# Attention of the first two blocks written as one pipeline ahead of the layers' loop

## The chip, the cores and the metric

One core of a Trainium2 chip runs the whole program. The metric is the device time of one execution in microseconds (us): 1756.26 us is the median of three runs of the kernel before (1754.75 to 1756.78). TensorE (PE) multiplies matrices, VectorE (DVE) and ScalarE (ACT) do elementwise work and read PSUM, GpSimd (POOL) does elementwise work in SBUF, SyncE (SP) issues most DMAs.

## The reference, cut to what matters

```python
# q, k, v: (batch 8, heads 8, seq 576, head_dim 64)
q_s = exp(q - max over d); q_s = q_s / (sum over d + 1e-9)
k_s = exp(k - max over s); k_s = k_s / (sum over s + 1e-9)
kv = einsum('bhsd,bhse->bhde', k_s, v)
x = einsum('bhsd,bhde->bhse', q_s, kv)      # -> (4608 tokens, 512)
h = relu(x @ w_in); x2 = (h * h) @ w_out    # d_ff 2048
xn = x2 / rms(x2) * rms_g
out = (silu(xn @ w_gate) * (xn @ w_val)) @ w_out2   # d_ff 1536
```

The keys' softmax runs over the sequence, the queries' over the 64 elements of a head. The weights come as 64-bit floats and are converted on the chip to fp32; most products are made of three fp32r passes on operands split into a high part and a remainder.

## The kernel before, in words

Tokens are cut into nine blocks of 512 (`NB`), heads into four pairs (`NP`, called heads `hp` below). Block j needs the attention of batch j, and of batch j - 1 for its first tokens, since a batch has 576. For each head of a block the attention does: load k, q, v; keys: maximum over the sequence (`a_kmax`, a reduction on VectorE, then `a_kt`, `a_mc`, `a_kb` to bring it across partitions with two transposes on TensorE), subtraction (`a_ksub`, VectorE), exponential (`a_kexp`); queries: `a_qmax`, `a_qsub` (GpSimd for block 0, else VectorE), `a_qexp`, `a_qsum`, `a_qn`, four transposes (`a_qT`) and a split into two parts; `a_kv` multiplies keys and values (ten fp32 products, twenty instructions), `a_kvf` normalizes, a split makes `kvd`, and `a_x` gives the transposed x in three fp32r passes, which is split again for the layers (for blocks 0 and 1 by `split_by_pe`, with a product with minus the identity).

The first layer pair of a block runs over 16 units c (`FF1`): `p1_h` multiplies x with w_in's piece c (12 matmuls of 512 columns into `ps_h`), `p1_r` does relu and square on ScalarE, `p1_hi` and `p1_lo` split the result, and `p1_B`, two units later, multiplies it with w_out's piece c (12 matmuls into `acc`). Units run in the order `units`, block after block; the second layers of all blocks follow. For c of `AHEAD` = 8 and more, block 1's `p1_h` runs in block 0's unit, with the same weights.

`tick` (line 379) converts the weights as a pipeline of jobs: load (SP queue), `d_words` (ScalarE: two conversions `s` and `n`), `d_float` (three VectorE operations on `t`), `d_split` (ScalarE high part, VectorE remainder), and writes most pieces back to DRAM (`wd`) over ScalarE's queue; later units load them into a ring of seven tiles `ws` (`feed`). Eight pieces stay in SBUF (`w`). The w_in and w_out pieces are all converted during block 0.

The order: block 0's attention is written out as a string of steps (lines 1062 to 1070), with four ticks in it; block 1's attention is spread over block 0's units by `A_STEPS`; that of the later blocks over the units of the block before by `HALVES`, in half units, and block 2's starts in the second part of block 0. Before unit 16 the instructions of an engine may be reordered by the scheduler; from unit 16 on (`pinned`) they stand in program order. PSUM has eight banks: four `acc`, two `h`, two `a`.

Of the kernel before, what the change touches and what calls it, by code (L numbers as in the profile page):

```python
# [40 lines left out]
def attention_moe_kernel(  # L41
# [12 lines left out]
    nc = tc.nc  # L54
# [60 lines left out]


    turns = {"a": 0, "so": 0, "d": 0, "t": 0}

    def a_ps(j, hp, name):
        if j == 0:  # L120
            return ps_acc.tile([P, 512], F32, tag=f"acc{hp}", name=name)
        turns["a"] += 1
        return ps_a.tile([P, 512], F32, tag=f"a{turns['a'] % 2}", name=name)
# [84 lines left out]
    AHEAD = 8  # L208

    def ahead(j, key):  # L210
        return j == 1 and key[0] == "i" and key[1] >= AHEAD
# [41 lines left out]
    def d_words(key):  # L253
# [115 lines left out]
    for c in range(FF1):  # L369
        due["i", c] = c - 2.5  # L370
        due["o", c] = c
# [29 lines left out]
    def a_tile(j, hp, shape, tag, dtype=F32, bufs=2):  # L401
        if j > 0 or hp < 2:
            bufs = {"qT": 1, "kt": 3}.get(tag, bufs)
            return pools["a"].tile([P, *shape], dtype, tag=tag, name=tag, bufs=bufs)
        return pools["s"].tile([P, *shape], dtype, tag=f"{tag}{hp}", name=f"{tag}0", bufs=1)
# [110 lines left out]
    def a_kexp(j, hp):  # L516
# [3 lines left out]
        ke = pools["a"].tile([P, SF + 1, 2, D], F32, tag="ke", name="ke", bufs=1)  # L520
# [43 lines left out]
    def a_qT(j, hp):  # L564
        ps = a_ps(j, hp, "ps_q")
# [6 lines left out]
        if j > 1:  # L572
            qTs[j, hp] = ps
            return
        qT = a_tile(j, hp, [2, T], "qT", F32R)
        if j == 0 and hp + 1 < NP:
            split_by_pool(qT, ps)
        else:
            split(qT, ps, j)
        qTs[j, hp] = qT  # L580
# [17 lines left out]
    def a_kv(j, hp):  # L598
        if j >= B:
            return  # L600
        ps = a_ps(j, hp, "ps_kv")
# [14 lines left out]

    def a_kvd(j, hp):
        a_kvf(j, hp)
        if j < B:
            split(kvd[j % 2][hp], kvs.pop((j, hp)), j)  # L620
# [10 lines left out]
    def a_kvf(j, hp):  # L631
# [7 lines left out]
        f = pools["a"].tile([P, P], F32, tag="kvf", name="kvf")  # L639
# [10 lines left out]
    def a_kvn(j, hp):  # L650
        a_kv(j, hp)
        a_kvd(j, hp)

    def a_x(j, hp):
# [4 lines left out]
        for b, lo, hi in ((j - 1, 0, p0), (j, p0, P)):  # L659
            if lo == hi:  # L660
# [6 lines left out]
                j > 1 or lo == 0,  # L667
                True,
                j,
                j < 2,  # L670
            )
        if j < 2:
            xts[j, hp] = xp.tile([P, 2, T], F32R, tag="x", name="x")
            split_by_pe(xts[j, hp], ps, j)
        else:
            xts[j, hp] = ps
# [23 lines left out]
    def p1_A(j, c):  # L700
        if not ahead(j, ("i", c)):
            kept[j, c] = p1_h(j, c)
            if j == 0:
                kept[j, c] = p1_r(kept[j, c], gp, 2)
        if j == 0 and c >= AHEAD:
            kept[1, c] = p1_r(p1_h(1, c), pools["r"], FF1 - AHEAD)
        if not ahead(j, ("i", c)):
            used(("i", c))

    def p1_hi(j, c):  # L710
        r = kept.pop((j, c))
        if j > 0 and not ahead(j, ("i", c)):
# [287 lines left out]
    for j in range(1, NB):  # L1000
        for hp in range(NP):
            for n, (at, f) in enumerate(A_STEPS if j == 1 else HALVES):
                if j == 1:
                    at = 2 * ((-6, -4, -2, 0)[hp] + at) + 1
                else:
                    at += (j - 1) * 2 * FF1 - 11 + 2 * FF1 // NP * hp
# [184 lines left out]
```

## Time and profile before

| | us |
|---|---|
| median of three runs | 1756.26 |
| the profiled execution | 1756.28 |
| its span, first to last instruction | 1754.3 |
| TensorE busy in the span | 1713.2 |
| VectorE busy | 1065.3 |
| ScalarE busy | 766.4 |

The span is the time from the first to the last instruction of the profiled execution; 2.0 us of its time lie around it. Busy times of TensorE count a matmul from start to its modelled end, so that a chain of matmuls is measured from start to start. An operation is named by its output and inputs, `out<-in`; all operations stand on line 34 (a helper), so they are told apart by their tiles: `ps_h` and `acc` are the layers' PSUM tiles, `ps_kt`, `ps_kb`, `ps_kv`, `ps_q`, `ps_x` the attention's, `t`, `s`, `n`, `raw` the weights' conversion, `ws` and `w` weights.

### The profile page before, as it was taken

The page shows a single profiled execution, that of the slowest core. Times are in us where ns is not written, and L with a number is a line of the kernel's source. Part 1 is how long each engine was busy: PE and PEld are TensorE (multiplying, and loading weights), DVE is VectorE, ACT ScalarE, POOL GpSimd, SP SyncE. Part 2 cuts the span into 40 slices and gives each one's busy share as a digit, 9 for nine tenths or more (in the row PEclk, how much of TensorE's full clock was granted, in tenths as well). Part 3 has the DMA queues.
Part 4 walks back from the last instruction along what each step waited for, and adds up shares of the span by engine and source line. Part 5 has one row for each costly group of instructions (what it writes and reads, how often), then busy time and mean ns, then how long its engine had stood idle before and what let it go on. Part 6 is the DMA issues. An engine that isn't in the chain of part 4 may idle for free.

```text
span 1754.3 us, 22975 instructions
## 1 busy us (share of the span) xinstructions
PE 1713.2 (98%) x8338; PEld 1412.2 (81%) x8338; DVE 1065.3 (61%) x1866; ACT 766.4 (44%) x1351; POOL 151.3 (9%) x166
## 2 busy tenths in 40 slices
PE   5899999999999999999999999999999999999998
PEld 3678888878888887888888888888888888888997
DVE  7986465556656555432465887657766775756444
ACT  4677434455555455543544335232532343223121
POOL 2000000222323232220000000000000000000000
PEclk9999999999999999999999999999999999999999
DMA  6777657779888887766556567666766666666885
GB/s 186 241 273 283 195 156 228 244 224 301 269 272 279 279 254 241 231 204 222 173 179 209 188 199 258 198 209 200 252 205 208 201 213 218 209 200 193 291 302 199
DMA packets 184511, 398.41 MB, mean 227 GB/s; under 512 B 57424, under 2 KB 96336, under 8 KB 183248
## 3 DMA queue, kind: packets, MB, share of 16 engines
q1 hardware_dynamic: 156368, 356.05, 62.5%
q10 hardware_dynamic: 28032, 40.90, 6.7%
q8 instruction: 67, 1.10, 0.3%
q14 instruction: 44, 0.36, 0.1%
HBM read 337.12 MB, written 59.77 MB: 226 GB/s over the span
## 4 chain that ended last, share of the span: by engine, by line
PE 94%; DVE 3%; DMA 1%; issue 1%; ACT 1%; SPq 0%; POOL 0%; ACTq 0%; DVEq 0%; POOLq 0%
PE acc L34 38%; PE ps_h L34 21%; PE ps_x L34 10%; PE ps_y L34 8%; PE ps_v L34 8%; PE ps_w L34 4%; PE ps_kv L34 2%; PE ps_q L34 1%; DVE t L34 1%; DMA vt<-in_v 1%; DVE mk L34 0%; DVE kt L34 0%; DVE qs L34 0%; DMA x2d<-e 0%; DMA kt<-in_k 0%
## 5 line engine op out<-in xcount | busy, mean ns | idle before, releaser
L34 PE MATMUL ps_h<-x,ws 128*128 128x512 f32 x1296 | 322.2, 398 | 4.0 <-DVE ws L34 2.6
L34 PE MATMUL acc<-g,ws 128*128 128x512 f32 x1296 | 315.2, 392 | 0.4 <-DVE ws L34 0.4
L34 PE MATMUL acc<-ws,g 128*128 128x512 f32 x1296 | 313.4, 390 | 1.0 <-ACT g L34 0.9
L34 PEld LDWEIGHTS ps_h<-x,ws 128*128 128x128 f32 x1296 | 240.9, 190 | 56.2 <-DVE ws L34 3.9
L34 PEld LDWEIGHTS acc<-g,ws 128*128 128x128 f32 x1296 | 241.9, 188 | 52.8 <-DVE ws L34 1.5
L34 PEld LDWEIGHTS acc<-ws,g 128*128 128x128 f32 x1296 | 241.4, 188 | 51.3 <-ACT g L34 2.1
L34 ACT ACTIVATE g<-r 128x512 fp32r<-128x512 f32 x252 | 158.7, 631 | 230.5 <-DVE r L34 226.0
L34 DVE TENSOR_TENSOR g<-r,g 128x512 fp32r<-128x512 f32 x252 | 172.5, 684 | 122.0 <-ACT g L34 120.3
L34 ACT ACTIVATE r<-ps_h 128x512 f32<-128x512 f32 x144 | 85.8, 597 | 243.0 <-PE ps_h L34 239.8
L34 PE MATMUL ps_y<-xo,ws 128*128 128x512 f32 (+1 forms) x720 | 168.6, 369 | 0.0
L34 PE MATMUL ps_v<-xo,ws 128*128 128x512 f32 (+1 forms) x720 | 168.4, 368 | 0.0
L34 PE MATMUL ps_x<-xo,ws 128*128 128x512 f32 (+1 forms) x720 | 167.5, 368 | 0.5 <-ACT p L34 0.5
L34 PEld LDWEIGHTS ps_x<-xo,ws 128*128 128x128 f32 x720 | 127.9, 188 | 24.4 <-ACT p L34 0.9
L34 PEld LDWEIGHTS ps_v<-xo,ws 128*128 128x128 f32 x720 | 127.7, 188 | 23.4
L34 PEld LDWEIGHTS ps_y<-xo,ws 128*128 128x128 f32 x720 | 126.4, 189 | 24.2 <-DVE sa L34 1.5
L34 PE MATMUL ps_h<-x,w 128*128 128x512 f32 x432 | 109.4, 402 | 0.9 <-DVE w L34 0.9
L34 PE MATMUL acc<-g,w 128*128 128x512 f32 x432 | 104.9, 392 | 1.0 <-ACT w L34 1.0
L34 PEld LDWEIGHTS ps_h<-x,w 128*128 128x128 f32 x432 | 81.2, 192 | 18.5 <-DVE w L34 1.3
L34 PEld LDWEIGHTS acc<-g,w 128*128 128x128 f32 x432 | 80.5, 188 | 18.7 <-ACT w L34 1.4
L34 ACT ACTIVATE r<-r 128x512 f32<-128x512 f32 x144 | 90.2, 631 | 3.7
L34 DVE TENSOR_TENSOR u<-ps_y,p 128x512 f32<-128x512 f32 (+1 forms) x120 | 76.0, 633 | 23.0 <-PE ps_y L34 21.5
L34 ACT ACTIVATE sg<-silu 128x512 f32<-128x512 f32 (+1 forms) x90 | 51.5, 585 | 83.6 <-DVE silu L34 83.4
(105 smaller groups left out, 1835.2 us busy)
## 6 DMA issues: line engine op xcount, KB each, us to landing
ws<-wd_t SPq DMA_DIRECT2D x210, 512.0 KB, 4.1
ws<-wd_u SPq DMA_DIRECT2D x108, 512.0 KB, 4.3
ws<-wd_o SPq DMA_DIRECT2D x96, 512.0 KB, 4.4
ws<-wd_i SPq DMA_DIRECT2D x89, 512.0 KB, 4.2
wd_t<-so ACTq DMA_DIRECT2D x84, 256.0 KB, 4.5
raw<-in_w_out SPq DMA_DIRECT2D x28, 512.0 KB, 4.7
raw<-in_w_gv SPq DMA_DIRECT2D x24, 512.0 KB, 5.7
x2d<-e SPq DMA_DIRECT2D x36, 256.0 KB, 2.9
```

Source lines behind the costliest of these rows:

```text
L34: ins = f(*args, **kw)
```

## The change

The attention of blocks 0 and 1 is done for all eight heads before the layers' loop, in nine written rounds, in program order on every engine (`pinned` is true from the start). Keys are transposed on TensorE (`s_kT`, four transposes), their maximum is a reduction along the free axis straight from PSUM (`s_km`), the exponential takes it as a bias (`s_ke`), and the result is transposed back (`s_kb`, five transposes) and copied to SBUF (`s_kc`). The 64 keys left over of each batch are transposed for all heads at once (`s_left`). Queries are copied once in fp32 (`s_qc`, no split), x is one fp32 product with the fp32 kv (`s_x`), and its remainder is made by the product with minus the identity (`s_xn`). The queries' subtraction moves to GpSimd for block 1 too. Block 2's boundary part gets its `kvd` split in units 8 to 11 of block 0.

Then block 0's units run by `unit_of_0`, with two ticks in each; block 1's first layer runs beside ten of them instead of eight (`AHEAD`). Each tick's split is cut in `d_hi` and `d_lo`, with the conversion of another weight between; the conversion `s` of w_in's pieces moves from ScalarE to VectorE. Weights are due one unit later. Block 2's attention starts two half units later. Keys of blocks 0 and 1 are loaded in pieces of 256 bytes and in the order p, c, h, d. Five ticks lie in the rounds 3 to 7. The rest of the program is the same.

```diff
-    AHEAD = 8
+    AHEAD = (1, 3, 5, 7, 9, 11, 12, 13, 14, 15)
...
-        if key[0] in ("i", "o"):
+        if key[0] == "o":
             se.activation(out=s, in_=hi, func=AF.Copy, scale=2.0**-112)
         else:
-            ge.tensor_scalar(
+            eng = ve if key[0] == "i" else ge
+            eng.tensor_scalar(
...
-    def d_split(key):
+    def d_hi(key):
         t = slot_tile(key) if key in res1 else ring_tile()
-        w_split(t, floats.pop(key), ve)
+        se.activation(out=t[:, 0], in_=floats[key], func=AF.Copy)
+        wt[key] = t
+
+    def d_lo(key):
+        t = wt[key]
+        ve.tensor_tensor(
+            out=t[:, 1], in0=floats.pop(key), in1=t[:, 0].bitcast(F32), op=ALU.subtract
+        )
         if key not in res1:
-            send(key, t, 2)
-        wt[key] = t
+            send(key, t, 1)
...
-        due["i", c] = c - 2.5
-        due["o", c] = c
+        due["i", c] = c - 1.5
+        due["o", c] = c + 0.5
...
-    def tick():
+    def tick(between=None):
         n = ticks[0]
-        for stage, ahead in ((d_split, 0), (d_float, 1), (d_words, 2), (d_load, 4)):
-            if 0 <= n - 4 + ahead < len(jobs):
-                key = jobs[n - 4 + ahead]
-                if key is None:
-                    continue
-                if stage == d_split and n - 4 + ahead >= NJ1:
-                    stage = d_quad
-                stage(key)
+        w1 = ((d_hi, 0), (d_float, 1), (d_lo, 0), (d_words, 2), (d_load, 4))
+        w2 = ((d_quad, 0), (d_float, 1), (d_words, 2), (d_load, 4))
+        for stage, ahead in w1 if n < NJ1 + 4 else w2:
+            if between and stage == d_words:
+                between()
+            if 0 <= n - 4 + ahead < len(jobs) and jobs[n - 4 + ahead] is not None:
+                stage(jobs[n - 4 + ahead])
         ticks[0] += 1
         if n < NJ1 + 4:
...
+    A_BUFS = {"kt": (3, 1), "qt": (3, 1), "vt": (2, 2), "qn": (2, 0), "ke": (1, 1), "qT": (1, 0)}
...
-        eng = ve if j > 0 else ge
+        eng = ve if j > 1 else ge
...
+    def s_left(j):
+        ps = lefts[j] = s_ps("h", "ps_l")
+        kl = kls.pop(j)
+        for hp in range(NP):
+            src = kl[:, hs_(hp), :].rearrange("p h d -> p (h d)")
+            te.transpose(ps[:, hp * SR : (hp + 1) * SR], src, ident[0:SR, 0:SR])
+        lmax[j] = s_tile([P, NP], "lm", 2)
+        ve.tensor_reduce(
+            out=lmax[j],
+            in_=ps[:, 0 : NP * SR].rearrange("p (n s) -> p n s", n=NP),
+            axis=AX.X,
+            op=ALU.max,
+            negate=True,
+        )
+
+    def s_kT(j, hp):
+        ps = kT[j, hp] = s_ps(f"acc{hp % 2}", "ps_kt")
+        kt = s_chunks(kts.pop((j, hp)))
+        for c in range(SF):
+            src = kt[:, c].rearrange("p h d -> p (h d)")
+            te.transpose(ps[:, c * P : (c + 1) * P], src, ident)
+
+    def s_km(j, hp):
+        m = s_tile([P, 2], "m", 2)
+        ve.tensor_reduce(out=m[:, 0:1], in_=kT[j, hp], axis=AX.X, op=ALU.max, negate=True)
+        ve.tensor_tensor(
+            out=m[:, 1:2], in0=m[:, 0:1], in1=lmax[j][:, hp : hp + 1], op=ALU.min
+        )
+        mks[j, hp] = m
+
+    def s_ke(j, hp):
+        ek = eks[j, hp] = s_tile([P, S], "ek", 2)
+        m = mks.pop((j, hp))[:, 1:2]
+        se.activation(out=ek[:, 0 : SF * P], in_=kT.pop((j, hp)), func=AF.Exp, bias=m)
+        se.activation(
+            out=ek[:, SF * P : S],
+            in_=lefts[j][:, hp * SR : (hp + 1) * SR],
+            func=AF.Exp,
+            bias=m,
+        )
+
+    def s_kb(j, hp):
+        ek = eks.pop((j, hp))
+        ps = kT[j, hp] = s_ps(f"acc{hp % 2}", "ps_kb")
+        for c in range(SF):
+            te.transpose(ps[:, c * P : (c + 1) * P], ek[:, c * P : (c + 1) * P], ident)
+        ps = kvs[j, hp] = s_ps("a0", "ps_kv")
+        te.transpose(ps[0:SR, P : 2 * P], ek[:, SF * P : S], ident)
+
+    def s_kc(j, hp):
+        ke = kes[j, hp] = a_tile(j, hp, [SF + 1, 2, D], "ke")
+        se.activation(
+            out=ke[:, 0:SF].rearrange("p c h d -> p (c h d)"), in_=kT.pop((j, hp)), func=AF.Copy
+        )
+        ve.tensor_copy(
+            out=ke[0:SR, SF].rearrange("p h d -> p (h d)"), in_=kvs[j, hp][0:SR, P : 2 * P]
+        )
+
+    def s_qc(j, hp):
+        f = qfs[j, hp] = s_tile([P, T], "qf", 2)
+        se.activation(out=f, in_=qTs.pop((j, hp)), func=AF.Copy)
+
+    def s_x(j, hp):
+        ps = xts[j, hp] = s_ps(f"acc{2 + hp % 2}", "ps_x")
+        qf = qfs.pop((j, hp)).rearrange("p (c t) -> p c t", c=NG)
+        p0 = min(j * OFF // NG, P)
+        view = ps.rearrange("p (c t) -> p c t", c=NG)
+        for b, lo, hi in ((j - 1, 0, p0), (j, p0, P)):
+            if lo < hi:
+                te.matmul(
+                    view[:, :, lo:hi],
+                    kvs[b, hp],
+                    qf[:, :, lo:hi],
+                    start=lo == 0,
+                    stop=True,
+                    skip_group_check=True,
+                )
+
+    def s_xh(j, hp):
+        split_hi(xts, (j, hp), xp.tile([P, 2, T], F32R, tag="x", name="x"))
+
+    def s_xn(j, hp):
+        t, ps = xts[j, hp]
+        te.matmul(ps, neg_r, t[:, 0], start=False, stop=True, skip_group_check=True)
+
+    def s_xl(j, hp):
+        t, ps = xts[j, hp]
+        se.activation(out=t[:, 1], in_=ps, func=AF.Copy)
+        xts[j, hp] = t
...
+    def p1_ahead(c):
+        kept[1, c] = p1_h(1, c)
+        used(("i", c))
+
+    def p1_ahead_r(c):
+        kept[1, c] = p1_r(kept[1, c], pools["r"], len(AHEAD))
...
-                    at += (j - 1) * 2 * FF1 - 11 + 2 * FF1 // NP * hp
+            for n, (at, f) in enumerate(HALVES):
+                at += (j - 1) * 2 * FF1 - (9 if j == 2 else 11) + 2 * FF1 // NP * hp
...
+        a_qmax(0, 0)
+        s_left(0)
+        a_qsub(0, 0)
+        at_(s_kT, 0)
+        ROUND = (
+            (s_km, 0),
+            (a_kv, -1),
+            (a_qexp, 0),
+            (s_ke, 0),
+            (a_kvf, -1),
+            (a_qT, -1),
+            (a_qmax, 1),
+            (a_qsub, 1),
+            (s_xh, -2),
+            (a_loadk, 4),
+            (s_kb, 0),
+            (s_kT, 1),
+            (s_xn, -2),
+            (a_qsum, 0),
+            (s_qc, -1),
+            (s_xl, -2),
+            (s_x, -1),
+            (s_kc, 0),
+            (a_qn, 0),
+            (a_loadq, 4),
+            (a_loadv, 2),
+        )
+        pending = []
+        last = []
+        beside = []
+
+        def unit_of_0(c):
+            p1_A(0, c)
+
+            def evict():
+                for x in last:
+                    p1_hi(*x)
+                if c == 1:
+                    at_(s_xl, len(heads) - 1)
+                while beside:
+                    p1_ahead_r(beside.pop())
+
+            tick(evict)
+            while ticks[0] < n_ticks(c) - 1:
                 tick()
+            for x in last:
+                p1_lo(*x)
+            last[:] = [(0, c)]
+            if ahead(1, ("i", c)):
+                p1_ahead(c)
+                beside.append(c)
+            pending.append((0, c))
+            while len(pending) > LAG:
+                p1_B(*pending.pop(0))
+            if beside:
+                tick(lambda: p1_hi(0, c))
+                p1_lo(0, c)
+                last.clear()
             else:
-                for f in first[step[0]]:
-                    f(0, int(step[1]))
+                tick()
+
...
+        for r in range(len(heads) + 1):
+            if r == 1:
+                s_loadl(1)
+            if r == 3:
+                s_left(1)
+            for f, at in ROUND:
+                at_(f, r + at)
+            if 3 <= r < 8:
+                tick()
+        at_(s_xh, len(heads) - 1)
+        unit_of_0(0)
+        at_(s_xn, len(heads) - 1)
+        unit_of_0(1)
...
+            if j == 0:
+                unit_of_0(c)
+                if 8 <= c < 8 + NP:
+                    a_kvd_hi(1, c - 8)
```

## Rows read from the trace of the kernel before

**Rows 1.** The page's chain that ended last, by engine.
```profile
PE 94%; DVE 3%; DMA 1%; issue 1%; ACT 1%; SPq 0%; POOL 0%; ACTq 0%; DVEq 0%; POOLq 0%
```

**Rows 2.** Windows: stretch, length, five engines' busy us (instructions), granted clock, DMA share, GB/s.
```profile
0.00:40.00 40.00, 18.91 (x117) 13.70 (x118) 31.13 (x74) 18.35 (x36) 10.12 (x26) 1.00 0.73 200
40.00:100.00 60.00, 51.15 (x256) 38.76 (x256) 56.44 (x124) 43.83 (x85) 0.35 (x3) 0.91 0.75 243
100.00:130.00 30.00, 29.73 (x147) 23.43 (x146) 22.91 (x42) 23.39 (x46) 0.12 (x1) 1.00 0.76 258
130.00:251.00 121.00, 121.00 (x633) 98.96 (x632) 70.37 (x143) 64.02 (x119) 0.47 (x4) 1.00 0.68 223
```

**Rows 3.** Windows of TensorE's instructions on tile ps_h alone, to 130 us.
```profile
0.00:130.00 130.00, 44.43 (x158) 0.96 0.75 233
```

**Rows 4.** The same of tile acc.
```profile
0.00:130.00 130.00, 27.57 (x108) 0.96 0.75 233
```

**Rows 5.** Timeline of TensorE at the end of block 1: start, length, what.
```profile
237.60 5.70 PE L34 MATMUL acc<-g,ws 128*128 128x512 f32 x24
243.14 1.02 PE L34 MATMUL ps_x<-qT,kvd 128*128 128x128 f32 x6
...
246.90 0.60 PE L34 MATMUL ps_q<-ident,qn 128*128 128x128 f32 x4
247.25 2.98 PE L34 MATMUL acc<-g,ws 128*128 128x512 f32 x12
250.16 0.95 PE L34 MATMUL ps_kv<-vt,ke 128*64 128x65 f32 x20
251.04 3.03 PE L34 MATMUL ps_h<-x,w 128*128 128x512 f32 x12
```

**Rows 6.** Timeline of TensorE in block 0's attention.
```profile
18.79 1.09 PE L34 MATMUL ps_q<-ident,qn 128*128 128x128 f32 x4 [3.98 <-DVE qs L34]
19.67 0.42 PE L34 MATMUL ps_kb<-ident,mcb 128*128 128x128 f32 x1
...
21.20 1.55 PE L34 MATMUL ps_kv<-vt,ke 128*64 128x65 f32 x20
22.68 0.48 PE L34 MATMUL ps_kb<-ident,mcb 128*128 128x128 f32 x1
```

**Rows 7.** VectorE's groups, 0 to 130 us: count | busy us, mean ns | idle before.
```profile
L34 DVE CUSTOM_DVE_ANT_0 t<-t,n 128x1024 uint16<-128x1024 uint16 x23 | 16.6, 728 | 1.0
L34 DVE SCALAR_TENSOR_TENSOR t<-s,t 128x512 uint32<-128x512 uint32 x23 | 15.6, 686 | 0.4
...
L34 DVE TENSOR_REDUCE mk<-kt 128x128 f32<-128x512 f32 x10 | 10.4, 1041 | 3.8 <-DMA kt<-in_k 3.7
L34 DVE TENSOR_SCALAR t<-s 128x512 uint32<-128x512 uint32 x23 | 9.4, 418 | 1.3 <-ACT s L34 0.4
...
L34 DVE TENSOR_REDUCE qm<-qt 128x8 f32<-128x512 f32 x10 | 6.8, 676 | 1.0 <-DMA qt<-in_q 0.9
L34 DVE TENSOR_TENSOR qn<-qt,qs 128x512 f32<-128x512 f32 x8 | 6.3, 789 | 1.0 <-PE ps_q L34 1.0
...
L34 DVE SCALAR_TENSOR_TENSOR kvf<-ps_kv,rk,mask 128x128 f32<-128x128 f32 x8 | 2.7, 340 | 0.0
...
L34 DVE TENSOR_REDUCE mc<-ps_kt 128x1 f32<-128x128 f32 x8 | 2.2, 280 | 0.9 <-PE ps_kt L34 0.9
...
L34 DVE RECIPROCAL qs<-qs 128x8 f32<-128x8 f32 x8 | 1.5, 189 | 0.0
```

**Rows 8.** ScalarE's groups, 0 to 130 us.
```profile
L34 ACT ACTIVATE n<-raw 128x512 int32<-128x512 uint32 x24 | 15.9, 661 | 0.0
...
L34 ACT ACTIVATE x<-ps_x 128x512 fp32r<-128x512 f32 x16 | 9.5, 593 | 11.9 <-PE ps_x L34 11.9
```

**Rows 9.** GpSimd's groups, 0 to 130 us.
```profile
L34 POOL TENSOR_TENSOR qt<-qt,qm 128x512 f32<-128x512 f32 x4 | 4.2, 1058 | 8.6 <-DVE qm L34 8.6
```

**Rows 10.** Loads of raw weights, 60 to 180 us, from issue to landing.
```profile
DMA to landing us min/median/max: 3.2/4.9/8.5
```

More of the change, by code (lines that the diff above doesn't have):

```diff
@@ L571, in a_qT @@
                 held(j, ins)
[L572 to L580, printed above, removed]
+        qTs[j, hp] = ps
     def split_hi(parts, key, dst):
@@ L615, in a_kv @@
         kvs[j, hp] = ps
[L617 to L620, printed above, removed]
     def a_kvd_hi(j, hp):
@@ L648, in a_kvf, with s_ps, s_chunks, s_loadl @@
         kvs[j, hp] = f
-    def a_kvn(j, hp):
-        a_kv(j, hp)
-        a_kvd(j, hp)
+    def s_ps(tag, name):
+        pool = ps_acc if tag[:3] == "acc" else ps_h if tag == "h" else ps_a
+        return pool.tile([P, 512], F32, tag=tag, name=name)
+    lefts, lmax, kls, qfs, kT, eks = ({} for _ in range(6))
+    def s_chunks(kt):
+        t = kt.rearrange("p h c d -> p (h c d)")[:, 0 : 2 * SF * D]
+        return t.rearrange("p (c h d) -> p c h d", c=SF, h=2)
+    def s_loadl(j):
+        kls[j] = s_tile([SR, 2 * NP, D], "kl", 1)
+        nc.sync.dma_start(out=kls[j], in_=k[j, :, SF * P : S, :].rearrange("h p d -> p h d"))
@@ L702, in p1_A @@
             kept[j, c] = p1_h(j, c)
[L703 to L708, printed above, removed]
+            if not (j == 0 and ahead(1, ("i", c))):
+                used(("i", c))
+    def p1_ahead(c):
+        kept[1, c] = p1_h(1, c)
+        used(("i", c))
+    def p1_ahead_r(c):
+        kept[1, c] = p1_r(kept[1, c], pools["r"], len(AHEAD))
     def p1_hi(j, c):
         r = kept.pop((j, c))
-        if j > 0 and not ahead(j, ("i", c)):
+        if not ahead(j, ("i", c)):
             r = p1_r(r, gp, 2)
@@ L1034, in attention_moe_kernel, with at_ @@
             )
-        for hp in range(NP):
-            a_loadk(0, hp)
-            a_loadq(0, hp)
-            if hp == 0:
-                make_identity(nc, ident)
-                ge.tensor_scalar(
-                    out=neg_r, in0=ident, scalar1=-1.0, scalar2=0.0, op0=ALU.mult, op1=ALU.add
-                )
-        for hp in range(NP):
-            a_loadv(0, hp)
+        heads = [(j, hp) for j in range(2) for hp in range(NP)]
+        pinned[0] = True
+        def at_(f, r):
+            if 0 <= r < len(heads):
+                f(*heads[r])
+        a_loadk(0, 0)
+        make_identity(nc, ident)
+        ge.tensor_scalar(
+            out=neg_r, in0=ident, scalar1=-1.0, scalar2=0.0, op0=ALU.mult, op1=ALU.add
+        )
+        s_loadl(0)
+        for f, hp in zip(
+            (a_loadq, a_loadk, a_loadq, a_loadv, a_loadk, a_loadq, a_loadv, a_loadk, a_loadq),
+            (0, 1, 1, 0, 2, 2, 1, 3, 3),
+        ):
+            f(0, hp)
         ge.memset(ones_r.bitcast(F32), 1.0 / DM)
@@ L1050, in attention_moe_kernel @@
         nc.sync.dma_start(out=g_sb, in_=rms_g.rearrange("(m p) -> p m", p=P))
-        first = {
-            "m": (a_kmax,),
-            "q": (a_qmax, a_qsub, a_qexp),
-            "n": (a_qsum, a_qn),
-            "r": (a_ktr,),
-            "e": (a_kb, a_ksub, a_kexp),
-            "t": (a_qT,),
-            "v": (a_kv, a_kvd),
-            "x": (a_x,),
-        }
-        for step in (
-            "m0 q0 n0 m1 m2 w q1 m3 n1 w q2 n2 q3 n3 r0 e0 r1 t0 r2 r3 e1 t1 v0 e2 w t2 e3 t3 "
-            "v1 v2 v3 w w x0 x1 x2 x3"
-        ).split():
-            if step == "w":
-                tick()
-            else:
-                for f in first[step[0]]:
-                    f(0, int(step[1]))
+        a_qmax(0, 0)
@@ new lines, in attention_moe_kernel @@
+        s_left(0)
[23 more added lines that the diff above has]
+            (a_loadv, 2),
+        )
@@ L1105, in attention_moe_kernel @@
             attention(2 * i)
-            pending.append((j, c, None))
+            pending.append((j, c))
+            while beside:
+                p1_ahead_r(beside.pop())
             while len(pending) > (LAG + 1 if j > 0 and c == LAG else LAG):
-                p1_B(*pending.pop(0)[:2])
+                p1_B(*pending.pop(0))
             for x in last:
```

93 lines of the change are left out of this document (40 added, 53 removed).

## The prediction

> **What bounds the kernel now.** I read the page's chain first, then windows, then single rows. The chain that ended last is 94% TensorE [rows 1], so a change counts only where TensorE is not streaming the layers' matmuls. The windows say where that is [rows 2]: from 130 to 251 us TensorE is busy all 121 us, with VectorE at 70 and ScalarE at 64; before 40 us it is busy 18.9 of 40. From 40 to 100 VectorE is the full engine, 56.4 of 60. To 130 us only 158 + 108 = 266 of the layers' matmuls have run [rows 3, 4]. At the end of block 1, 24 of them take from 237.60 to 243.14, 0.231 us each [rows 5], so 266 are 61.4 us of work. The other 68.6 us went to the attention of blocks 0 and 1 and to waiting for it. That is what the change acts on. Block 2's first layer starts at 251.04 [rows 5]; from there both kernels do the same, so the end moves as this mark does. The profiled execution took 1756.28 us, 1.98 more than its span, and is 0.02 above the median of the three runs.
>
> With S the time at which the layers' matmuls start in a stream, the new mark is S + 61.4 + 121 + stalls: the 266, then all that ran from 130 to 251, block 2's attention included. Before, S and the stalls stood for 68.6.
>
> **VectorE in a round.** Each head costs: maximum from PSUM, bounded by the 128-column reduction from PSUM, 0.28, and the 512-element one with 128 results, 1.04 [rows 7]; I take 0.68, as `qm` with as many elements and few results. Its small minimum 0.15 (no more than the reciprocal's 0.19). `a_kvf` 0.15 + 0.15 + 0.34. `a_qmax` 0.68. `a_qsum` 0.68 + 0.15 + 0.19. The copy of the keys left over, 0.2 to 0.34, take 0.28. `a_qn` 0.68 (its mean of 0.79 holds one stretched case). Sum 4.13 us. Gone are the 1.04 + 0.28 of the old maximum, the transposed maximum's 0.28 + 0.3, the keys' subtraction near 0.95, kvd's remainder, and for block 1 the query subtraction and split, 0.68 each. Four heads of 6.3 and four of 7.6, 55.6 in all, become 33; against this 16 conversions at 0.42 come from ScalarE, 6.7. A change of k's load to 256-byte pieces, two tiles more for k and q, and the SP issues of a round (one k, two q, three v, some 3.5 us) I cost at nothing: k and q are loaded four heads ahead, v two. Without that cover a late load costs its lateness, and behind it on SP stand the next round's loads and the raw weights.
>
> **TensorE in a round.** Thirteen transposes, `a_kv`, x and the product with minus the identity. Four transposes take 0.88 us at 18.79 and 0.35 at 246.90, `a_kv` 1.48 at 21.20 and 0.88 at 250.16 [rows 5, 6]: the lower of the two clock levels (1.2 GHz) early, the higher (2.4) late, though the page prints 1.00 for the first 40 us [rows 2], for which it has no event. The fp32 x has no row. From below: three passes of 512, 0.69 high. From above: 1024 columns at `a_kv`'s 0.88 per 650, 1.39. I take two instructions of four transposes' length, 0.70 high and 1.76 low. Sum: 13 x 0.088 + 0.88 + 0.70 + 0.23 = 2.95 high; 2.86 + 1.48 + 1.76 + 0.46 = 6.56 low.
>
> **The other engines in a round.** ScalarE six full passes of about 0.6 [rows 8] and 64 more columns (0.1 to 0.59, take 0.3), 3.9. GpSimd one subtraction of 1.06 [rows 9], behind which only the next exponential stands. So at the higher level VectorE paces the rounds, at the lower one TensorE does. I add 0.3 for `a_kv`, which waits for `s_kc`, itself behind `s_xl` on ScalarE: 4.4 us per round. The fifth transpose of `s_kb` needs the bank that the previous head's `a_kvf` reads; behind it on TensorE stands the next head's `s_kT`. That wait is inside the 4.4 as long as `a_kvf` is early.
>
> **When the stream starts.** VectorE's reductions waited 3.7 us for k and 0.9 more for q [rows 7]; with the transposes and the left-over keys the first `s_km` is at about 6.4 (4.6 to 8). Round 0 is a chain: maximum 0.83, exponentials 0.9, nine low transposes 2.0, copy 0.28, `a_qn` 0.68, so 4.7; round 1 the same; round 2 half at either level, 5.5. `s_km` of the fourth head: 21.3. Four rounds of 4.4 and the ticks' VectorE work (a reduction 0.4, two conversions 0.42, one float 0.42 + 0.69 + 0.73 = 1.83), 3.1: 42.0. The last round without a query maximum 3.5, its tick 1.83 + 0.68, `a_kvf` 0.65, x and the remainder 0.93: 49.6. S = 50.
>
> **Block 0's units.** VectorE per unit: two floats 3.66, three remainders of 0.68, one conversion 0.42, 6.1. TensorE 24 matmuls, 5.5, or 36 in ten units, 8.3: mean 7.3. ScalarE 5 to 6.3, from its passes of 0.59 to 0.66. TensorE paces. In units 10 to 15 block 2's attention adds VectorE 8.3 per head and four units, about 2.1: 8.2 against TensorE's 8.4. That is nearly equal, so I charge 3 us (0 to 10). The stream may begin at the lower level, at most 12 x 0.23 = 2.8; I charge 1. The later start of block 2's attention puts its last split behind the last `p1_B` before the mark, 2.8 us that hide ScalarE 0.6 and VectorE 0.7; uncovered, 1.3. The kvd splits in units 8 to 11 hide there too.
>
> Sum: 50 + 61.4 + 121 + 4 = 236.4, 14.6 us before 251.0: 1756.28 - 14.6 = 1741.7.
>
> **Rivals.**
> First, the clock stays low through the rounds, TensorE paces them, and most of the gain is gone. From 15.8 us five rounds of 6.56 give 48.6, the last head's products 12.5 more: S = 61. With 2.8 at the stream's start the mark is 249 and the time 1754.6. For it: in all of the first 40 us, with transposes and `a_kv` at up to half of TensorE's time, nothing ran at the higher level [rows 2, 6]. Against: there TensorE had gaps, while these rounds leave none, and 40 to 100 granted 0.91 with TensorE busy 51 of 60. The Trainium skill says this too (TensorE: Matmul & The Clock Gate, Part 4: PE-mode transpose): transposes do not release the clock as matmuls do. By that rule the time would be this rival's. No row before has a dense run of transposes, so the trace neither agrees nor speaks against it.
>
> Second, written order makes waits add up: a round is 5.5, not 4.4. Seven rounds cost 7.7 more: 1749.4. For it: each engine's next step stands behind another's; against: every chain I can write down is shorter than VectorE's sum.
>
> Third, slower: raw weights come too late. Loads are issued two ticks ahead, 7.3 us at the new pace; landings took 4.9 in the median and 8.5 at most [rows 10], at a DMA share of 0.75 [rows 2]. The same bytes pass in less time. If the mean landing reached 8.5, the conversion on ScalarE and all evictions behind it would wait 1.2 us in each of 16 units: 19.2 lost, 1760.9. It turns to a loss from 7.3 + 14.6/16 = 8.2 us.
>
> Fourth, block 1 does not get shorter: ten of its units hold 12 matmuls and attention, some 3.4 us, while DMA must bring 512 KB of w_out and some 190 of k, q, v, 3.2 us at 223 GB/s [rows 2]. Should that bind by 1 us in ten units, the time is 1751.7.
>
> **How the numbers follow.** Chances: forecast 0.58, first rival 0.17, second 0.12, third 0.08, fourth 0.05. The forecast's own range is 1735 (S = 45, no stalls) to 1749 (stalls of 11). The range given, 1735 to 1757, takes in the first, second and fourth and leaves the third out. A measurement of this kernel tells about 0.2%, 3.5 us, from no change, so faster means under 1752.7: the forecast, 0.10 of the second, 0.05 of the first, and the fourth's half, 0.02, give 0.75. Slower 0.09, mostly the third; the rest, 0.16, is the same.
>
> **What would show it.** The mark, block 2's first `ps_h<-x,w`, near 236; the first `ps_h` at 50; VectorE near full from 20 to 50 with eight `s_km` reductions 4.4 us apart and near 0.68 each; four transposes at 0.35 rather than 0.88 after 20 us; TensorE without waits from 55 on, at most 3 us of them between units 10 and 15. The forecast is wrong if the transposes stay at 0.88, if TensorE waits for VectorE's `ws` or ScalarE's `n` between 60 and 170, or if the mark falls by less than 4 us.

## The result, and the profile after

The kernel after takes 1734.77 us (median of four runs, 1733.5 to 1736.88) against 1756.52 beside it: a ratio of 0.9879, with a 95% interval of 0.9862 to 0.9896. The forecast was 1741.7. So the sign and most of the size were right, the change gave 7 us more than the sum, and the median lies 0.2 us under the low end of the range.

The profiled execution after took 1733.5 us with a span of 1731.5, 22.8 shorter than before. From its page, the busy times and the chain by engine [rows 1]:

```profile
PE 1707.3 (99%) x8390; PEld 1410.3 (81%) x8390; DVE 1059.1 (61%) x1847; ACT 763.4 (44%) x1336; POOL 151.8 (9%) x167
...
PE 95%; DVE 2%; ACT 1%; SPq 0%; DMA 0%; issue 0%; POOL 0%; DVEq 0%; POOLq 0%; ACTq 0%
```

The chain was already 94% TensorE and has one point more: as in [rows 1], the ends of the work are TensorE's. Of the 22.8 us, 16.9 were idle time of TensorE (41.1 us of the span before, 24.2 after), and in 5.9 it was busy (1713.2 before, 1707.3 after). The windows, with the columns of [rows 2] and the stretches cut to the new stages:

```profile
0.00:20.00 20.00, 11.84 (x88) 9.19 (x88) 12.29 (x31) 8.72 (x16) 6.00 (x22) 1.00 1.02 206
20.00:50.00 30.00, 24.55 (x222) 16.55 (x221) 27.87 (x73) 23.36 (x47) 4.39 (x8) 1.00 0.83 219
50.00:70.00 20.00, 19.34 (x84) 15.23 (x83) 18.39 (x33) 17.62 (x32) 0.00 (x0) 1.00 0.96 316
70.00:130.00 60.00, 60.00 (x266) 49.67 (x266) 55.10 (x100) 47.51 (x86) 0.00 (x0) 1.00 0.88 305
130.00:231.50 101.50, 101.50 (x549) 83.21 (x547) 61.24 (x127) 49.84 (x92) 1.72 (x6) 1.00 0.67 222
```

Where [rows 2] had TensorE at 51 of 60 us from 40 to 100, it is now busy 60.00 of 60 from 70 to 130. VectorE, at 55.1 of these 60, is nearly as full as before and yet holds up nothing. The layers' matmuls that have run by 130 us, on `ps_h` and then on `acc`:

```profile
0.00:130.00 130.00, 55.08 (x231) 1.00 0.90 272
...
0.00:130.00 130.00, 28.82 (x120) 1.00 0.90 272
```

That is 351, where [rows 3, 4] had 266. TensorE's timeline (start, length, what), from the first rounds to the mark:

```profile
10.35 1.06 PE L34 MATMUL ps_kt<-ident,kt 128*128 128x128 f32 x4
11.34 1.55 PE L34 MATMUL ps_kv<-vt,ke 128*64 128x65 f32 x20
...
14.57 0.60 PE L34 MATMUL ps_kt<-ident,kt 128*128 128x128 f32 x4
15.01 1.02 PE L34 MATMUL ps_x<-qf,kvf 128*128 128x512 f32 x2
...
48.61 3.27 PE L34 MATMUL ps_h<-x,w 128*128 128x512 f32 x12
...
231.52 3.04 PE L34 MATMUL ps_h<-x,w 128*128 128x512 f32 x12
```

Four transposes take 0.99 us from start to start at 10.35 (0.88 in [rows 6]), and 0.44 at 14.57: in between, at 14.3 us, the granted clock went from 1.2 to 2.4 GHz, and in this execution it stayed there to the end. The stream starts at S = 48.61 (forecast 50), and the mark, block 2's first `ps_h<-x,w`, falls at 231.52, 19.5 before the 251.04 of [rows 5] (forecast 14.6). Between them lie 182.91 us: the 61.4 + 121 of the sum and only 0.51 of stalls.

The remaining 3.3 of the 22.8 us come after the mark, where the sum had nothing. There TensorE runs the same 7188 matmuls in the same order in both kernels. About 1.6 of the 3.3 belong to one place in block 3, where in both TensorE waits some 3.3 us for `x`, before and then after:

```profile
366.95 0.63 PE L34 MATMUL ps_q<-ident,qn 128*128 128x128 f32 x4 [3.28 <-DVE x L34]
...
347.28 0.63 PE L34 MATMUL ps_q<-ident,qn 128*128 128x128 f32 x4 [3.25 <-DVE x L34]
```

The windows around it, before:

```profile
360.00:380.00 20.00, 16.72 (x88) 13.32 (x87) 9.90 (x18) 9.05 (x17) 5.31 (x5) 0.91 0.77 253
```

and after:

```profile
340.00:360.00 20.00, 16.75 (x95) 13.47 (x95) 11.15 (x20) 9.43 (x19) 5.31 (x5) 1.00 0.83 265
```

TensorE is busy 16.7 of 20 us in both, but before the clock then fell for 3.4 us (0.91 in the mean), and in this execution it did not. It is chance, not the change: of the twelve runs below, all with the change in some form, each waits there for 3.2 to 3.3 us and has that low stretch, once (1501.3 to 1502.1 us from mark to end) or for twice as long (1502.9 to 1503.0); after's 1500.03 is the one without it. Of the other 1.6 us, 0.7 go with one more wait in the kernel before, in the second layers:

```profile
PE ps_x L34 <- ACT p L34: 0.5, 1, 0.5
```

About 0.4 lie behind the last matmul, and the rest is in pieces of under 0.1 us.

### The profile page after: what moved, and what is told of

It reads as the page before. It is cut to its first block, busy times and chain, and to the rows that moved or that the text cites. A ratio compares the mean times of both kernels' runs of the same rounds, so it can differ in the third digit from the quotient of the medians.

```text
span 1731.5 us, 23049 instructions
## 1 busy us (share of the span) xinstructions
PE 1707.3 (99%) x8390; PEld 1410.3 (81%) x8390; DVE 1059.1 (61%) x1847; ACT 763.4 (44%) x1336; POOL 151.8 (9%) x167
## 4 chain that ended last, share of the span: by engine, by line
PE 95%; DVE 2%; ACT 1%; SPq 0%; DMA 0%; issue 0%; POOL 0%; DVEq 0%; POOLq 0%; ACTq 0%
PE acc L34 39%; PE ps_h L34 22%; PE ps_x L34 10%; PE ps_y L34 9%; PE ps_v L34 8%; PE ps_w L34 4%; PE ps_kv L34 1%; DVE t L34 1%; PE ps_q L34 1%; PE ps_kb L34 0%; PE ps_kt L34 0%; DVE qs L34 0%; PE ps_s L34 0%; DMA qt<-in_q 0%; DMA vt<-in_v 0%
## 5 line engine op out<-in xcount | busy, mean ns | idle before, releaser
L34 PE MATMUL ps_h<-x,ws 128*128 128x512 f32 x1296 | 316.6, 394 | 0.7 <-ACT r L34 0.7
L34 PEld LDWEIGHTS ps_y<-xo,ws 128*128 128x128 f32 x720 | 126.4, 189 | 24.2 <-DVE sa L34 1.5
L34 PEld LDWEIGHTS acc<-g,w 128*128 128x128 f32 x432 | 80.7, 188 | 16.9
```

The costliest lines, as they stand in the source:

```text
L34: ins = f(*args, **kw)
```

## The experiments

Each edit is against the kernel after, one run unless the table tells more; the kernel before took 1754.5 to 1756.2 beside them. Read of each are S, the mark, and the stages of S: the first `s_km` (`m<-ps_kt`), the time from the first to the eighth (the rounds), and from the eighth to S (the tail). After has 7.10, 34.06 and 7.45.

| run | us | first | rounds | tail | S | S to mark |
|---|---|---|---|---|---|---|
| after | 1734.77 (4 runs) | 7.10 | 34.06 | 7.45 | 48.61 | 182.91 |
| e1 | 1736.38 | 7.23 | 33.41 | 8.24 | 48.88 | 183.83 |
| e2 | 1739.28 | 8.00 | 34.86 | 8.46 | 51.32 | 182.90 |
| e3 | 1736.29 | 7.13 | 33.77 | 8.54 | 49.44 | 183.11 |
| e4 | 1744.71 | 7.59 | 33.92 | 9.40 | 50.91 | 190.14 |
| e5 | 1740.47 | 7.70 | 34.17 | 8.57 | 50.44 | 186.43 |
| e6 | 1737.46 | 7.19 | 33.59 | 8.62 | 49.40 | 183.26 |
| e7 | 1749.12 | 7.22 | 43.18 | 11.97 | 62.37 | 182.59 |
| e8 | 1734.38 | 6.96 | 32.30 | 8.58 | 47.84 | 183.43 |
| e9 | 1738.83 (4 runs) | 7.23 | 34.69 | 10.27 | 52.19 | 182.87 |
| e10 | 1737.32 (4 runs) | 7.19 | 34.69 | 7.95 | 49.83 | 182.87 |
| e11 | 1741.28 | 7.14 | 37.24 | 10.27 | 54.65 | 182.90 |
| e12 | 1733.23 (4 runs) | 7.28 | 32.00 | 7.50 | 46.78 | 182.90 |

Two columns carry a scatter that is not the edit's. The first `s_km` moves by up to a microsecond with the first loads. The tail splits by the clock: 7.45 to 7.95 where it stays high, 8.24 to 8.62 with one low stretch of 3.4 us between 42 and 49, 9.4 to 10.3 with a double one (e7 apart, which has two low stretches). So a microsecond of a single run's time, or of its S, tells nothing by itself. The rounds scatter less: e4, whose edit leaves them alone, has 33.92 against 34.06. S to the mark scatters by up to 0.9: e1, which leaves the units alone, has 183.83, with a wait of 1.3 us for ScalarE's `r` where after has 0.3.

**e1: does VectorE alone pace the rounds?**

```diff
-        ve.tensor_scalar_add(out=qs, in0=qs, scalar1=1e-9)
+        if j > 1:
+            ve.tensor_scalar_add(out=qs, in0=qs, scalar1=1e-9)
```

> Leaves out the addition of 1e-9 to the queries' sums in blocks 0 and 1. Theory: VectorE paces the rounds, and GpSimd's subtraction, which now runs beside the small addition in every round, holds that addition up (0.55 us mean in the changed kernel, 0.15 before). Without it VectorE saves 0.55 in each of eight rounds: the stream of the layers' matmuls starts at 44.2 instead of 48.6, and block 2's first matmul moves from 231.5 to 227.1. Rival A: only the 0.15 goes, since the reciprocal behind it is held up in its place: start 47.4, mark 230.3. Rival B: a chain over the engines paces the rounds, not VectorE: start 48.6, mark 231.5.

These additions are the surprise of the page after. VectorE's groups by shape, 0 to 48 us (count | busy us, mean ns):

```profile
L34 DVE TENSOR_REDUCE m<-ps_kt 128x1 f32<-128x512 f32 x8 | 5.5, 681 | 0.0
L34 DVE TENSOR_SCALAR qs<-qs 128x8 f32<-128x8 f32 x8 | 4.4, 552 | 0.3
```

The reduction from PSUM took 0.681, as forecast, but eight additions on 128 x 8 took 4.4 us. Seven of them lie between the first and the eighth `s_km`, 4.2 us in all; `qn`, which now falls beside GpSimd's work, took back 0.8 (0.67 to 0.82 us each). That leaves 3.4, but the rounds are only 0.65 shorter. What VectorE waited for, 11 to 48 us (total us, times, longest), in e1:

```profile
DVE rk L34 <- PE ps_kv L34: 2.0, 4, 0.7
DVE ke L34 <- PE ps_kv L34: 1.0, 1, 1.0
DVE s L34 <- DMA raw<-in_w_in: 0.7, 1, 0.7
DVE kes L34 <- PE ps_kv L34: 0.5, 1, 0.5
```

and in after:

```profile
DVE rk L34 <- PE ps_kv L34: 0.8, 2, 0.6
```

The rest turned into waits for `a_kv` and `s_kb` and, 0.7 us of it, for a raw weight. The reciprocal, which now runs beside GpSimd's subtraction in the addition's place, took 0.20 in both runs, so nothing moved to it (rival A). So VectorE's sum is not what alone paces a round: the chain through TensorE lies a few tenths behind it.

**e2: what holds the small addition?** In after's timeline it ends within 0.1 us of GpSimd's subtraction, which had begun before it. The eighth, which has no subtraction beside it, is short (last line):

```profile
14.44 1.04 POOL L34 TENSOR_TENSOR qt<-qt,qm 128x512 f32<-128x512 f32 x1 [4.50 <-DVE qm L34]
14.99 0.58 DVE L34 TENSOR_SCALAR qs<-qs 128x8 f32<-128x8 f32 x1
...
43.31 0.17 DVE L34 TENSOR_SCALAR qs<-qs 128x8 f32<-128x8 f32 x1
```

```diff
-        eng = ve if j > 1 else ge
+        eng = ve
```

> The queries' subtraction of blocks 0 and 1 on VectorE instead of GpSimd. Theory (VectorE paces the rounds, GpSimd holds up its small addition): 0.68 more and 0.40 less in each of eight rounds, 2.2 in all: start of the stream 50.8, mark 233.7, and the small addition back at 0.15. Rival A (the addition is long for another reason): 5.4 more, start 54.0, mark 236.9, the addition still 0.55. Rival B (a chain paces the rounds): start 48.6.

With the subtraction on VectorE the addition is back at what [rows 7] allowed a small operation:

```profile
L34 DVE TENSOR_SCALAR qs<-qs 128x8 f32<-128x8 f32 x8 | 1.4, 172 | 0.3
```

So GpSimd's operation held it. The forecast S came out, but partly by luck: of the 2.7 us the rounds carry 0.8, the first load 0.9 and the clock 1.0 (the tail). In seven rounds VectorE got 4.8 us of subtractions more (0.68 each) and 3.0 of additions less, 1.8 in all, and 0.8 of it shows: here too a round has some room on VectorE.

**e3: what raises the clock?** Unread transposes of the identity in the first microseconds:

```diff
+        ps = s_ps("a1", "ps_w")
+        for c in range(18):
+            te.transpose(ps[:, c % 4 * P : (c % 4 + 1) * P], ident, ident)
         s_left(0)
...
         at_(s_kT, 0)
+        for c in range(9):
+            te.transpose(ps[:, c % 4 * P : (c % 4 + 1) * P], ident, ident)
```

> 27 extra transposes of the identity, whose result nobody reads, 18 before the first transposes of keys and 9 behind them, so that TensorE does nothing but transposes from 1.4 to about 9 us. Theory (transposes release the clock as matmuls do): the higher level from 7.5 to 10 us on instead of 14.3, round 0 and 1 lose some 2 us of low-level work, start of the stream 47 to 48. Rival, the skill's rule (transposes do not count): the level rises no sooner than 14.3, and the start is at 48.6 or later by what the extra transposes hold up.

TensorE's timeline in e3:

```profile
1.35 4.10 PE L34 MATMUL ps_w<-ident 128*128 128x128 f32 x18 [1.35 <-POOL ident masks.py:199]
...
6.00 1.09 PE L34 MATMUL ps_kt<-ident,kt 128*128 128x128 f32 x4
6.92 1.16 PE L34 MATMUL ps_w<-ident 128*128 128x128 f32 x9
...
9.83 0.60 PE L34 MATMUL ps_kt<-ident,kt 128*128 128x128 f32 x4
...
20.17 0.46 PE L34 MATMUL ps_l<-ident,kl 64*128 64x64 f32 x4 [0.72 <-DMA kl<-in_k]
```

Eighteen transposes at 1.35 take 4.10 us, 0.228 each; nine at 6.92 take 1.16, 0.129. The granted clock rose at 6.9 us, when TensorE had run nothing but transposes; in the other twelve traces of the change it rose between 12.6 and 18.9. The Trainium skill (TensorE: Matmul & The Clock Gate, Part 4: PE-mode transpose) says that in transpose mode the higher clock "doesn't engage"; this trace disagrees, and the measurement decides. (The trace prints these transposes as MATMUL and does not tell their mode.) But the clock that rose 7.4 us earlier made the rounds only 0.3 shorter. From `s_km` to `s_km` the first two took 3.97 and 4.32 (4.35 and 5.03 in after), but the third 5.59 (4.80): there TensorE stood 0.72 us for block 1's left-over keys (last line), which the earlier clock had only brought forward.

**e4: is the spread of block 1's first layer worth anything?** Eight neighbouring units, as before, instead of ten spread ones:

```diff
-    AHEAD = (1, 3, 5, 7, 9, 11, 12, 13, 14, 15)
+    AHEAD = (8, 9, 10, 11, 12, 13, 14, 15)
```

> Block 1's first layer beside units 8 to 15 of block 0 alone, as before the change, instead of ten spread units. Theory: units 0 to 7 then hold 24 matmuls, 5.5 us, against 6.1 of VectorE, so VectorE paces them and TensorE waits 0.6 to 1 us in each: 5 to 8 us, mark 236.5 to 239.5. Rival: the two units fewer in block 0 come back in block 1 at the same price and the weights are ready in time: mark 231.5.

S to the mark is 7.2 longer. TensorE's waits from 48.5 to 150 us in e4:

```profile
PE ps_h L34 <- DVE ws L34: 3.2, 6, 1.4
PE ps_h L34 <- ACT r L34: 1.4, 1, 1.4
...
PE ps_h L34 <- DVE w L34: 0.4, 1, 0.4
```

In after there is one such line:

```profile
PE ps_h L34 <- ACT r L34: 0.7, 2, 0.3
```

In units with 24 matmuls TensorE is through in 5.5 us, and VectorE with 6.1 us of conversion is the later one. The waits behind VectorE end at 59.0, 65.1, 71.2, 77.4, 83.5, 89.6 and 95.7, 6.1 us apart: VectorE paces these units. Spreading gives every other unit 36 matmuls, so that VectorE's lateness does not add up over neighbours. The forecast charged its stalls to units 10 to 15; the ones that the spread avoids stand in units 0 to 7.

**e5: how much room has VectorE in the units?** The remainder of each w_out piece (one per unit, 0.68) is computed twice:

```diff
+        if key[0] == "o":
+            ve.tensor_tensor(
+                out=t[:, 1], in0=floats[key], in1=t[:, 0].bitcast(F32), op=ALU.subtract
+            )
```

> Every remainder of a w_out piece is computed twice on VectorE, 0.68 us more in each of block 0's 16 units. In the changed kernel TensorE has no wait from 70 to 130 us while VectorE is busy 9.0 to 9.7 of 10. Theory (VectorE has about 0.4 of a unit's 7.3 us left): some 0.3 per unit comes through, mark 234 to 237.5. Rival A (nothing left, as the prediction's charge for the last six units supposed): 0.68 per unit, mark 242. Rival B (the busy share hides more room): mark 231.5 to 233, the start of the stream at 48.6 to 51 in each case.

S to the mark grew by 3.5, 0.22 per unit of 0.68 added: the room is about 0.46 us per unit in the mean. It is not the same everywhere: TensorE's waits end at 59.8, 66.5 and 70.0, then at 133.4 and 151.1, and none lies between. Most are for ScalarE's `r`, up to 0.9 at a time (48.5 to 150 us):

```profile
PE ps_h L34 <- ACT r L34: 1.7, 3, 0.9
```

**e6: the conversion that moved.** w_in's conversion `s` back to ScalarE:

```diff
-        if key[0] == "o":
+        if key[0] in ("i", "o"):
```

> The conversion s of w_in's pieces back on ScalarE: VectorE 0.42 less and ScalarE 0.66 more in each unit of block 0. Theory (TensorE paces block 0, ScalarE with 5.7 + 0.66 of 7.3 us still has room): from the start of the stream to the mark nothing changes (182.4 to 184). Rival (ScalarE, in written order with evictions behind the conversions, becomes the pace): 0.3 to 0.6 per unit, 187 to 192 from start to mark.

183.26 against 182.91, within the scatter: the conversion's move neither helped nor hurt in the units.

**e7: q and x in fp32.** q^T split in two parts again and x by three passes, with the key products' split written into the rounds (and so no longer in units 8 to 11):

```diff
-        f = qfs[j, hp] = s_tile([P, T], "qf", 2)
-        se.activation(out=f, in_=qTs.pop((j, hp)), func=AF.Copy)
+        qfs[j, hp] = a_tile(j, hp, [2, T], "qT", F32R)
+        split(qfs[j, hp], qTs.pop((j, hp)), j)
+
+    def s_kd(j, hp):
+        split(kvd[j % 2][hp], kvs.pop((j, hp)), j)
...
+            (s_kd, -1),
             (s_x, -1),
```

> q and kv of blocks 0 and 1 split into two parts again and x made in three fp32r passes; everything else as in the changed kernel. Per head VectorE does 0.68 + 0.28 more, ScalarE 0.3 more, TensorE 0.2 less. Theory (VectorE paces the rounds): start of the stream 7.7 later, 56.3, mark 239. Rival A (the rounds wait for chains and SP, VectorE has some 0.5 of a round to give): start 52 to 53. Rival B (the shorter x pays for it): start 48.6 or earlier.

The mark is 13.4 later, against an expected 7.7. The rounds are 9.1 longer, 1.3 each, and the tail 4.5, with the clock low for 10.2 us from 53.6. TensorE's largest wait from 6 to 135 us:

```profile
PE ps_x L34 <- DVE qT L34: 10.4, 8, 1.9
```

and the window of the rounds:

```profile
20.00:62.00 42.00, 30.17 (x236) 21.81 (x234) 35.95 (x90) 25.38 (x53) 5.50 (x10) 0.86 0.68 181
```

VectorE's remainder sits between the transposed q and x in the written order, and TensorE stops for it in each of the eight heads; the clock fell twice (0.86 in the mean). In this written order, going without the fp32 form thus costs 13.4 us, by a wait more than by VectorE's sum, which is not even full here (35.95 of 42). Whether the remainder costs less at another place in the round was not tried.

**e8: several waits at once.** The q and k additions gone for blocks 0 and 1, v in one DMA, the left-over keys of block 1 loaded at the start, the first keys' transposes ahead of `s_left`:

```diff
+        if j < 2:
+            nc.sync.dma_start(
+                out=vt[:, 0:SF, :, 0:D],
+                in_=v[j, hs, 0 : SF * P, :].rearrange("h (p c) d -> p c h d", c=SF),
+            )
...
+            ve.reciprocal(out=rk, in_=ps[:, D : D + 1])
...
+        at_(s_kT, 0)
+        s_loadl(1)
```

> Four edits together, in blocks 0 and 1 only: both additions of 1e-9 left out, v of a head loaded with one DMA instead of two, the left-over keys of block 1 loaded at the start, and the first transposes of keys put ahead of those of the left-over keys. Theory (after the additions the rounds wait in turn for a_kv, for loads that SP issues late, and for the left-over keys): SP has 5 us less to issue, the waits of the run without the addition (4.2 us on VectorE) go by half, the first maximum is 0.7 earlier: start of the stream 45.5 to 46.5. Rival (the chain from a_kv over a_kvf to the next transposes paces the rounds alone): start 48 to 48.9, as without the addition.

The rounds are 1.8 shorter, less than VectorE's additions alone would save; S = 47.84 lies between the theory and its rival. VectorE's largest wait within the rounds:

```profile
DVE rk L34 <- PE ps_kv L34: 3.3, 6, 0.9
```

So what comes late next is `a_kv`, which stands between the copy of the keys and `a_kvf`.

**e9: that chain cut short.** e8, with the copy of the keys `s_kc` put right behind the next head's transposes (four runs):

```diff
             (s_kT, 1),
+            (s_kc, 0),
             (s_xn, -2),
...
-            (s_kc, 0),
```

> The four edits of the run with fewer waits, and in every round s_kc moved from behind s_xl to right behind the next head's transposes, so that a_kv does not wait on ScalarE for the remainder of an older head. Theory (what is left of a round is VectorE's wait for a_kv, 0.3 to 0.9 of 4.3 us): rounds of 3.9, start of the stream 46 to 46.8 instead of 47.8, mark 229.5 to 230.5, time 1732 to 1734. Rival (the wait moves to the next engine, as it did before): start 47.5 to 48, mark 231.

It went the other way: a ratio of 0.9904 (0.9889 to 0.9919), S 4.3 later than in e8, 2.4 of it in the rounds and 1.7 in the tail. VectorE's waits for `ps_kv`, 6 to 52 us:

```profile
DVE kes L34 <- PE ps_kv L34: 2.8, 3, 1.7
DVE rk L34 <- PE ps_kv L34: 2.3, 5, 0.6
DVE ke L34 <- PE ps_kv L34: 1.8, 2, 1.6
```

`s_kc` has a part on VectorE (the left-over keys), and at its new place this stands in VectorE's queue before the transposes it reads are done, with `a_qsum` and `a_qn` behind it. Neither the theory nor its rival had said so.

**e10, e12: the clock at 40 us.** The tails suggest that a pause of TensorE near 40 us lets the clock fall. Twenty unread transposes ahead of the queries' transposes of one late head, on e9 (e10) and on e8 (e12), four runs each:

```diff
+        if (j, hp) == (1, 2):
+            for c in range(20):
+                te.transpose(ps[:, c % 4 * P : (c % 4 + 1) * P], ident, ident)
```

> The same with 20 transposes of the identity, which nobody reads, ahead of the seventh head's query transposes, where TensorE stands still for 2 us beside VectorE's weight conversion. Theory (the clock fell between 36 and 54 us in six of seven runs because TensorE did little there, and the stream then began low or late): no low stretch between 40 and 52 us, start of the stream 0.5 to 1 us earlier than without them, mark 229 to 229.8. Rival (the fall has another reason, or the extra transposes hold up the chain): a low stretch all the same, start no earlier.

> The run with fewer waits (four edits, s_kc where the changed kernel has it) with the 20 unread transposes ahead of the seventh head's query transposes. Theory (TensorE's pause at 39 to 41 us lets the clock fall, and the last two heads' products then run at the lower level): no low stretch between 40 and 52 us, start of the stream 46.3 to 47.3 instead of 47.8, mark 229 to 230, time 1731.5 to 1734 and so 0.5 to 3 us under the changed kernel. Rival (the lower level costs nothing there, since VectorE ends the rounds): start 47.8, mark 231.3, time as the changed kernel.

The window 38 to 50 us, in e9:

```profile
38.00:50.00 12.00, 9.15 (x65) 5.74 (x64) 9.28 (x21) 7.83 (x15) 1.07 (x2) 0.74 0.59 180
```

in e10:

```profile
38.00:50.00 12.00, 10.36 (x93) 7.47 (x91) 10.25 (x24) 8.77 (x17) 1.03 (x2) 1.00 0.61 186
```

in e8:

```profile
38.00:50.00 12.00, 9.70 (x67) 6.31 (x63) 9.20 (x21) 8.43 (x18) 0.00 (x0) 0.86 0.55 174
```

and in e12:

```profile
38.00:50.00 12.00, 11.42 (x95) 8.78 (x91) 10.13 (x23) 9.62 (x20) 0.00 (x0) 1.00 0.69 216
```

The granted clock goes from 0.74 and 0.86 to 1.00. The eighth `s_km` is where it was within 0.04 us in both pairs, and S comes 2.35 and 1.06 earlier. So more work for TensorE made the stretch shorter. Each side is one trace: of the eleven traces of the change without these transposes ten have a fall that begins between 36 and 54 us (eight of nine when the expectation counted six of seven), of the two with them none. The mean clocks of all four runs point the same way: 0.996 to 0.997 in e9, 0.997 to 0.999 in e10. e12 came out as expected in S, mark and time. e10's mark, 232.70, is far from the expected 229 to 229.8, which was reckoned from e9's forecast. e12 has a ratio of 0.987 (0.9853 to 0.9886); its median of 1733.23 is the lowest, but its interval overlaps that of after, so the two are not told apart.

**e11: the copy moved alone**, on the kernel after.

> The changed kernel with s_kc moved alone, additions and loads as they are. Theory (with the additions VectorE has no wait to lose, 0.8 us over all the rounds): start of the stream within 0.5 of 48.6 where the clock stays high, up to 50 where it falls. Rival (the order on ScalarE sets the round): start 46 to 47.

The rounds are 3.2 longer and the double low stretch is back: 6.0 at S, where 0.5, or 1.4 with a low clock, was expected. At a high clock from round 1 on, e10 against e12, the copy's place costs 3.05 us at S. The rest lies in the tail, with the clock low for 6.8 us from 46.2. Why the stretch is a double one is not shown: e4, where the copy was not moved, has one too.

No run separates the rest of the change: the new form of the keys' maximum, the program order and the later due dates of the weights were not tested apart.

## Why the prediction was right, and where it was off

- **What bounds.** Right. The mark stands for the gain: 19.5 of the 22.8 us. From 70 us to the mark TensorE has no gap.
- **Start of the stream, 50.** Measured 48.61. By its own steps: first `s_km` 7.10 (6.4 taken), fourth head 21.28 (21.3), eighth 41.16 (42.0), tail 7.45 (8.0). The clock was high from 14.3 us, in round 1, where I took round 2 as half low. The rounds with ticks took 4.28 to 4.62 and 6.40, together 19.9 where 20.7 was taken. But 4.4 came near by errors that cancel. In the round from the fourth `s_km` VectorE has no gap:

```profile
21.28 0.68 DVE L34 TENSOR_REDUCE m<-ps_kt 128x1 f32<-128x512 f32 x1
...
24.02 0.63 DVE L34 TENSOR_SCALAR qs<-qs 128x8 f32<-128x8 f32 x1
...
25.56 0.68 DVE L34 TENSOR_REDUCE m<-ps_kt 128x1 f32<-128x512 f32 x1
```

Its operations add up to 4.59 us instead of 4.13, since the addition took 0.63 and not 0.15. They pass in 4.28, since six of them start some 0.08 us before the one ahead of them ends. And the 0.3 per round for `a_kv` came as only 0.8 in all rounds (e1's last view).
- **Stalls, 4.** This is the term that failed: 0.51. I charged 3 us for units 10 to 15 since 8.2 on VectorE is "nearly equal" to 8.4 on TensorE, and 1 for a low clock at the stream's start. Neither came: the clock was high when the stream began, and VectorE was not that full in these units (113.1 to 160.0 us):

```profile
113.10:160.00 46.90, 46.90 (x211) 38.71 (x210) 36.65 (x67) 31.12 (x56) 1.25 (x2) 1.00 0.80 285
```

That is 36.65 of 46.90, where the sum had 49.2 of 50.4. To 134.9 it is 20.78 of 21.80, so near equality did hold there for three units, and it cost nothing. From there on it is 15.87 of 25.10; the prediction put the same conversions into every unit.
- **"From there both kernels do the same, so the end moves as this mark does."** The work is the same, 7188 matmuls, but the time is off by 3.3: 1.6 by a low stretch that one profiled execution had and the other had not, 0.7 by one more wait before, 0.4 behind the last matmul.
- These three make the difference to the profiled execution: 1.4 + 3.5 + 3.3 = 8.2 = 1741.7 - 1733.5.
- **The range.** Its low end was worked out wrongly. S = 45 without stalls is a mark of 227.4, 23.6 before 251.04, and 1732.6 rather than 1735; that end would have held the median.
- **"At the higher level VectorE paces the rounds."** Too simple. VectorE is near full (27.87 of 30) and waits only 0.8 us for `a_kv` in all the rounds, but e1 took 3.4 us off it in seven rounds and won 0.65, and e2 added 1.8 and lost 0.8. VectorE's sum and the chain of a head lie within tenths of each other, and the written order decides which one is late. The sum gave nearly the right time because the two lie so near, and in part by luck (above).
- **The first rival** (clock low through the rounds) fell: 0.44 us for four transposes from 14.6 on, and e3 shows transposes alone raising the clock.
- **The second** (waits add up, 5.5 per round) did not come in this kernel, but it is real for its neighbours: one moved copy costs 3 us (e10 against e12, both with e8's edits), a remainder between q and x 1.3 per round (e7).
- **The third** (raw weights late) and **the fourth** fell. Landings, 60 to 140 us, in after:

```profile
DMA to landing us min/median/max: 3.4/5.5/8.5
```

The median rose from the 4.9 of [rows 10] at a DMA share of 0.88, but TensorE waited for no load behind them, and block 1's own units are part of the 101.5 of 101.5 us busy from 130 on. SP's issues, which the prediction costed at nothing, stood nearly back to back from 0.74 to 35.6 us (51 issues), but from 11 us on VectorE waited for none of them in the rounds.

## What to carry to other kernels

In a pipeline written in order on every engine, weigh each step by what stands behind it in its queue, not by its length: taking 3.4 us off the fullest engine won 0.65, moving one copy cost 3. Where two engines are nearly equal over a stretch, spread the extra work of the other one over the units before adding a stall to the sum (e4: 7.2 us). And give a profiled execution's time a look at its clock before it is compared at the level of a microsecond: one low stretch of 3.4 us cost 1.1 us at S (e8 against e12) and about 1.6 in block 3.

## What was not expected of the hardware

- A VectorE addition on 128 x 8 elements took 0.55 us while GpSimd subtracted (1.04 us), and 0.17 with GpSimd idle (e2).
- Transposes alone raised TensorE's granted clock, 6.9 us after the start, and with twenty unread ones it stayed up through a stretch where it fell without them (0.74 and 0.86 in the mean; two pairs of traces).
- The same code is granted the higher clock in one execution and not in another around the same pauses (near 45 and 350 us). The four runs of the kernel after line up by their mean clock: 1733.5 us at 1.000, 1734.26 and 1735.28 at 0.999, 1736.88 at 0.998. The profiled one is the fastest of them, and only it has a trace.
